# Softmax weights in a PSUM bank of their own, and GpSimd subtractions beside the products with v

## The chip, the cores and the metric

The kernel runs on one core of a Trainium2 chip. A core has a matrix engine (TensorE, PE in the profile), a vector engine (VectorE, DVE), an activation engine (ScalarE, ACT), a general engine (GpSimd, POOL) and a queue that issues transfers (SyncE, SP). TensorE writes its sums into PSUM, eight banks of 128 partitions with 512 fp32 values each; everything else works on SBUF, and transfers (DMA) go between SBUF and the chip's memory. The metric is the time of one execution on the device in microseconds (us), the median over several runs.

## The reference

The input x is 2048 x 640. Two branches are computed from it and mixed by a gate per row: attention with a short dilated window, and a dense layer, Mish and a second dense layer.

```python
def _A_ref(x, wqkv, wo):              # H = 32 heads of Dh = 20, W, dil = 8, 2
    qkv = (x @ wqkv).reshape(B, S, 3, H, Dh) ...
    idx = pos[:, None] - (arange(W) * dil)[None, :]      # 8 earlier rows, every second one
    logits = einsum("bhsd,bhswd->bhsw", q, k[idx]) * Dh ** -0.5   # -1e9 where idx < 0
    attn = softmax(logits, axis=-1)
    o = einsum("bhsw,bhswd->bhsd", attn, v[idx])
    return o.reshape(B, S, D) @ wo
def _B_ref(x, w1, b1, w2):            # F = 1728
    h = x @ w1 + b1
    return (h * tanh(softplus(h))) @ w2
g = sigmoid((x * gate_w).sum(-1))
return g * _A_ref(...) + (1 - g) * _B_ref(...)
```

## The kernel before, in words

**Precision.** Each fp32 matrix operand is split into a high and a low part, both in the format that TensorE takes at full speed: ScalarE copies it (the high part, line 345), and VectorE or GpSimd subtracts that from the original (the low part, line 348, function `split`). A tile "pair" holds both. One product is then three matmuls (`mm3`, lines 394 to 396): high by high, high by low, low by high. Some splits are made without a subtraction on an engine: ScalarE writes the negated copy and a transfer adds the source to it in flight (`split_added`, issued by GpSimd, line 357). Other additions in flight are issued by GpSimd too: those of the activations (`plus`, line 657) and of the results (`adding`, line 1066).

**Stages.** `qkv` forms q, k and v with x as the stationary operand, for 8 units u = 0..7: 4 groups of 8 heads (hq) times two halves of the rows (P). `mlp1` forms the first dense layer, and Mish is taken on ScalarE (line 669). In both, one PSUM bank takes 15 matmuls, and ScalarE drains it. `mlp2` is the second dense layer, in seven products named a, b, c, e, g, d, f that each run over seven blocks kc; a product keeps its accumulations in banks named p0, p1, q, u0, u1, w0, w1, r, v0, v1, for two halves P. `wo_first` and `wo_second` multiply the attention's result by wo, the first for row blocks tb 0 and 1, the second for tb 2 and 3. In `wo_second` five output blocks dc of tb 2 and the first three of tb 3 are begun with the operands kc 0 to 2, which are there early (`EARLY = 3`), then those of tb 2 are finished with kc 3 and 4, then the other two of tb 3 are begun, and then tb 3 is finished. `finish` adds a bank to the gated result of the other branch on VectorE (line 1282) and stores it.

**Attention** runs on VectorE beside the matmuls, function `attention`. Per unit there are two halves of four slots, and in each half: q by k for two slots at a time (line 451), the sum over a head's 20 elements (line 454, the kind "qk sum"), the maximum, the subtraction and the exponential on ScalarE, a copy of the weights into `pw` on ScalarE (`copied`, line 474), their sum, its reciprocal and the gate, and the scaling of `pw` by them (function `shares`, line 482). Then `outputs` multiplies v by the weights for two slots at a time (line 488, 2560 elements per partition, the weights repeated over a head's 20 elements), and three additions (lines 493, 494, 496) sum over the window. `out` transposes four slots (line 407) and stores them, for `wo_first` and `wo_second` to load.

**The order of the work** is worked out before the program is emitted, by a list planner (class `Plan`). Every piece of work is a task with an engine, an assumed duration, a rank and the tasks it waits for; the planner plays the engines forward and emits each task when it starts one. For each engine it takes the lowest rank among the ready tasks whose buffers are free; TensorE's tasks all have rank 0 and so go in the order written, past those that are not ready or have no free bank. Buffers come from rings, banks among them (`"bank": 8`). Attention has ranks from 2 - 0.6 on and comes behind the splits (`SOON` = 0, `NEXT` = 1).

Tasks of the engine "ANY" (most splits, and the sums of weight blocks of `sums_of`, lines 751 and 764) may go to VectorE or GpSimd. While attention is under way, VectorE takes one only when it is due: its matmul less than `NEAR` = 8000 ns off in TensorE's order, or, for tasks without one, after a wait (`PATIENCE`). GpSimd takes one only if it would end, by the planner's times, at most 150 ns after a "quiet" time, which is set when VectorE starts an instruction of the kind "qk sum". Whatever GpSimd starts in a quiet time, additions in flight included, is given a wait on the VectorE instruction ahead of the quiet one (`gate`, set through `follow`). The lines in `Plan.run`:

```python
fit = [t for t in fit if now + t.ns[0] <= quiet + 150 or t.rank <= -0.5]
...
if e == "POOL" and on and quiet > now and gate and ins:
    self.follow(ins, gate)
if e == "DVE":
    ...
    if t.kind == "qk sum":
        quiet, gate = now + t.ns, last
```

Of the kernel before, what the change touches and what calls it, by code (L numbers as in the profile page):

```python
# [8 lines left out]
F32 = mybir.dt.float32  # L9
F32R = mybir.dt.float32r  # L10
AF = mybir.ActivationFunctionType
OP = mybir.AluOpType
AX = mybir.AxisListType
PSUM = bass.MemoryType.PSUM
DRAM = bass.MemoryType.DRAM

S, D, H, DH, W, F = 2048, 640, 32, 20, 8, 1728
KC = D // 128
NQ, HQ = 4, 8
# [7 lines left out]
BIG = 1e9  # L27
WARM, WARM_TAIL = 6, 4
WA = 256

# [27 lines left out]
class Plan:  # L60


    NEAR, PATIENCE = 8000, 2000

    LAG = {"PE": 220, "ACT": 220, "DVE": 200, "POOL": 150, "SP": 3000}
    FAR, ROOM = 25000, 5000
# [29 lines left out]
    def run(self):  # L96
# [5 lines left out]
        quiet, gate, last, shared, begun = 0.0, None, None, [], False  # L102
# [33 lines left out]
        while left:  # L136
            again = not events or events[0][0] > now
            while again:
                again = False
                for e in self.LAG:  # L140
                    if busy[e]:
                        continue
                    fit = [t for t in ready[e] if fits(t)]
                    on = begun and loud
                    if e == "POOL":
                        fit += [t for t in shared if fits(t)]
                        if on:
                            fit = [t for t in fit if now + t.ns[0] <= quiet + 150 or t.rank <= -0.5]
                    elif e == "DVE":
                        fit += [t for t in shared if fits(t) and (not on or due(t))]  # L150
                    if not fit:
                        continue
                    t = min(fit, key=lambda t: t.key)
                    if t.both:
                        shared.remove(t)
                        t.eng = e
                    else:
                        ready[e].remove(t)
                    if type(t.ns) is tuple:
                        t.ns = t.ns[e == "DVE"]  # L160
                    for b in t.take:
                        b.ring.free -= 1
                        b.ring.at += 1
                        b.t = b.make()
                    t.start = now
                    ins = t.fn(e) if t.both else t.fn()
# [3 lines that stand above are left out]
                        if t.kind:  # L170
                            begun = True
                            loud -= 1
                        if t.kind == "qk sum":
                            quiet, gate = now + t.ns, last
                        last = ins or last
                    if e == "PE":
                        begun_pe = max(begun_pe, t.pos)
                    busy[e] = again = True
                    end = over = now + t.ns * self.CARE.get(e, 1.0)
                    heapq.heappush(events, (over, n, "idle", e))  # L180
                    if t.land:
                        wire = max(wire, end) + t.land
                        end = wire + (0 if e == "SP" else self.ADDING)
                    heapq.heappush(events, (end + self.LAG[e], n + 1, "done", t))
                    if e != "SP":
                        heapq.heappush(events, (over, n + 2, "own", t))
                    n += 3
            if not events:
                stuck = [(t.eng, t.rank, t.waits, getattr(t.fn, "__qualname__", "")) for e in ready for t in ready[e]]
                raise RuntimeError(f"nothing can go on at {now}, {left} left: {stuck[:20]}")  # L190
            now, _, what, x = heapq.heappop(events)
            if what == "idle":
                busy[x] = False
                continue
            if what == "ready":
                (shared if x.both else ready[x.eng]).append(x)
                continue
            if what == "done":
                left -= 1
                x.at = now  # L200
                for b in x.hold:
                    b.left -= 1
                    if not b.left:
                        b.ring.free += 1
                        if b.gone:
                            b.gone()
            for t in x.then:

                if (t.eng == x.eng and x.eng != "SP") != (what == "own"):
                    continue  # L210
                t.waits -= 1
                if not t.waits:
                    t.why, t.rdy = x, now
                    late = self.ROOM if x.eng == "SP" and t.eng == "ACT" and first[t] - begun_pe > self.FAR else 0
                    heapq.heappush(events, (now + max(t.late, late), n, "ready", t))
                    n += 1
# [4 lines left out]
def kernel(ctx: ExitStack, tc: tile.TileContext, x, wq, wo, w1, b1, w2, xt, gw, out):  # L221
    nc = tc.nc
    scale = DH ** -0.5
    V, G, A = nc.vector, nc.gpsimd, nc.scalar

    keep = ctx.enter_context(tc.tile_pool(name="keep", bufs=1))
    dram = ctx.enter_context(tc.tile_pool(name="dram", bufs=1, space=DRAM))
    psum = ctx.enter_context(tc.tile_pool(name="psum", bufs=8, space=PSUM))
    top = ctx.enter_context(tc.tile_pool(name="top", bufs=1, side="right"))
    pe = ctx.enter_context(tc.tile_pool(name="pe", bufs=1, side="right"))  # L230
    at = ctx.enter_context(tc.tile_pool(name="at", bufs=1))
# [1 line left out]
    NPAIR, NW, NRAW, NH = 21, 3, 7, 4  # L233
    def follow(ins, gate):
        tc.add_manual_dep(ins.ins, gate.ins.name,
                          mybir.DependencyInfo(mybir.DependencyClass.Sync, mybir.DependencyReason.DATA), reason="beside")

    plan = Plan({"bank": 8, "pair": NPAIR, "w": NW, "raw": NRAW, "raw1": 1, "hb": NH,
                 "ot": 1, "b": 11}, follow)

    def ps_buf():
# [75 lines left out]
    lg_w = lg.rearrange("p s h w -> p s w h")  # L317
    pw = at.tile([128, 8, W, HQ], F32, name="pw")
    pw_h = pw.rearrange("p s w h -> p s h w")
    pr = at.tile([128, 2, W, QF], F32, name="pr")  # L320
    mx = at.tile([128, 8, HQ], F32, name="mx")
    sm = at.tile([128, 8, HQ], F32, name="sm")
# [108 lines left out]
    def attention(u, P, hq, ready, gates):  # L431
# [44 lines left out]
        def shares(a, rank, e, copied):  # L476
            h = slice(a, a + 4)
            step = chain(rank)
            t = step("DVE", 415, lambda: V.tensor_reduce(sm[:, h], lg[:, h], op=OP.add, axis=AX.X), [e])
            step("DVE", 390, lambda: V.reciprocal(sm[:, h], sm[:, h]))  # L480
            step("DVE", 230, lambda: V.tensor_tensor(sm[:, h], sm[:, h], gate[:, P, h, None].to_broadcast([128, 4, HQ]), op=OP.mult), gates)
            return t, step("DVE", 430, lambda: V.tensor_tensor(pw[:, h], pw[:, h], sm[:, h, None, :].to_broadcast([128, 4, W, HQ]), op=OP.mult), [copied])

        def outputs(s0, rank, after):
            def mul():
                vw = window(kv, s0, 1)
                vw = bass.AP(tensor=vw.tensor, offset=vw.offset, ap=[list(d) for d in vw.ap[:3]] + [[DH, HQ], [1, DH]])
                V.tensor_tensor(pr.rearrange("p s w (h d) -> p s w h d", d=DH), vw,  # L488
                                pw[:, s0:s0 + 2, :, :, None].to_broadcast([128, 2, W, HQ, DH]), op=OP.mult)

            step = chain(rank)
            step("DVE", 2850, mul, after, kind="pv")
            step("DVE", 1495, lambda: V.tensor_tensor(pr[:, :, 0:4], pr[:, :, 0:4], pr[:, :, 4:8], op=OP.add), kind="pv")  # L493
            step("DVE", 855, lambda: V.tensor_tensor(pr[:, :, 0:2], pr[:, :, 0:2], pr[:, :, 2:4], op=OP.add), kind="pv")

            return step("DVE", 525, lambda: V.tensor_tensor(q[:, s0:s0 + 2], pr[:, :, 0], pr[:, :, 1], op=OP.add), kind="pv")
# [16 lines left out]
        for i, a in enumerate((4, 0)):  # L513
            h = 2 * u + i
# [3 lines left out]
            e, copied = softmax(a, LATER - 0.6, [bounded(a, a + 4, [t1, t2])], used)  # L518
            summed, w = shares(a, turn_of(h, 1), e, copied)
# [39 lines left out]
    def qkv(u, P, hq):  # L559
# [4 lines left out]
        if u == 0:  # L564
            last = warmed
            for kc in range(2):
                (xh, xl), (wh, wl) = X[0, kc].ready, WQ[0, kc].ready
                for a, b, w in ((0, 0, [xh, wh]), (0, 1, [wl]), (1, 0, [xl])):
                    slots = range(4)
                    if (kc, a, b) == (0, 0, 0):  # L570

                        for c0, c1, wc in ((0, WA, WQ[0, 0].first), (WA, n, wh)):
                            last = pe_add(2 * mm_ns(n // 2), lambda c0=c0, c1=c1: nc.tensor.matmul(
# [738 lines left out]
    def first_in():  # L1312
# [5 lines left out]
        WQ[0, 0] = wp  # L1318
        cols = ((0, WA), (WA, NCOL))
        d = [dma(lambda c0=c0, c1=c1: wr.t[:, c0:c1], lambda c0=c0, c1=c1: wq[0, 0][:, c0:c1], rank=-1.5, take=[wr] if not c0 else (),  # L1320
                 hold=[wr], size=(c1 - c0) * 512) for c0, c1 in cols]
        hi = [add("ACT", act_ns(WA), lambda: A.activation(wp.t[:, 0, :WA], wr.t[:, :WA], AF.Copy), d[:1], rank=SOON, take=[wp], hold=[wr]),
              add("DVE", 250, lambda: V.tensor_copy(wp.t[:, 0, WA:NCOL], wr.t[:, WA:NCOL]), d[1:], rank=-1.1, hold=[wr, wp])]
# [129 lines left out]
```

## Time and profile before

| what | us |
|---|---|
| median of 3 runs | 631.64 (631.42 to 632.35) |
| span of the profiled execution | 630.2 |
| TensorE busy | 625.6 (99%) |
| VectorE busy | 581.0 (92%) |
| ScalarE busy | 333.5 (53%) |
| GpSimd busy | 143.4 (23%) |

The profiled execution's own time is its span, 630.2 us from the first to the last instruction; the run's time has a little around that, and the median of the runs is 631.64 us. In the rows that follow, a group of instructions is named by its line, its engine, its operation and the tiles it writes and reads (out<-in), with count, busy time in us and the mean of one in ns; what stands after the second bar is the engine's idle time just before them. A row of waits names who waited for whom, the time in total, how often, and the longest. A row of the timeline begins with start and duration in us.

### The profile page before, as it was taken

How to read it: one execution, taken by the hardware profiler on the slowest of the kernel's cores; microseconds unless marked ns; L12 is line 12 of the kernel's file. 1: busy time of each engine (PE TensorE's matmuls, PEld its weight loads, DVE VectorE, ACT ScalarE, POOL GpSimd, SP SyncE). 2: the span in 40 equal slices, each digit the busy share in tenths (PEclk: the TensorE clock that was granted, in tenths of full speed). 3: DMA queues.
4: the chain of work that ended last, by engine and by line, in shares of the span. 5: the costliest groups of instructions: out<-in, count | busy, mean ns of one | idle time of the engine just before them, and what ended most of it. 6: DMA issues, size and time to landing. Idle time of an engine off the chain costs nothing.

```text
span 630.2 us, 8823 instructions
## 1 busy us (share of the span) xinstructions
PE 625.6 (99%) x2794; PEld 521.9 (83%) x2794; DVE 581.0 (92%) x610; ACT 333.5 (53%) x705; POOL 143.4 (23%) x154
## 2 busy tenths in 40 slices
PE   9999999999999999999999999999999999999997
PEld 6888888888888888888888888888888888888886
DVE  7699989999999998998999899999999989999934
ACT  6665764454536645353652626683765536666300
POOL 1321242232312332331333341211201010002320
PEclk9999999999999999999999999999999999999999
DMA  9999998999977998895898798899989867799985
GB/s 321 344 338 225 180 271 210 317 256 274 269 206 175 322 313 195 209 271 112 186 324 185 150 290 196 216 322 287 298 275 287 231 222 252 231 340 322 253 236 189
DMA packets 105694, 159.12 MB, mean 253 GB/s; under 512 B 13728, under 2 KB 52768, under 8 KB 105360
## 3 DMA queue, kind: packets, MB, share of 16 engines
q1 hardware_dynamic: 89648, 131.74, 64.1%
q0 software_dynamic: 15712, 26.56, 27.3%
q8 instruction: 22, 0.36, 0.2%
q10 hardware_dynamic: 288, 0.26, 0.1%
q14 instruction: 24, 0.20, 0.1%
HBM read 95.27 MB, written 67.51 MB: 258 GB/s over the span
## 4 chain that ended last, share of the span: by engine, by line
PE 98%; DMA 1%; ACT 0%; SPq 0%; DVE 0%; issue 0%
PE bank L395 32%; PE bank L394 32%; PE bank L396 32%; DMA hb<-in_x 1%; PE bank L400 1%; PE bank L401 1%; PE bank L546 0%; SPq L362 0%; ACT kvq L345 0%; ACT pair L345 0%; DVE kvq L1282 0%
## 5 line engine op out<-in xcount | busy, mean ns | idle before, releaser
L395 PE MATMUL bank<-pair 128*128 128x512 f32 (+1 forms) x500 | 193.1, 386 | 0.0
L394 PE MATMUL bank<-pair 128*128 128x512 f32 (+1 forms) x500 | 193.1, 386 | 0.0
L396 PE MATMUL bank<-pair 128*128 128x512 f32 (+1 forms) x500 | 193.1, 386 | 0.0
L396 PEld LDWEIGHTS bank<-pair 128*128 128x128 f32 x500 | 93.9, 188 | 18.1
L394 PEld LDWEIGHTS bank<-pair 128*128 128x128 f32 x500 | 93.9, 188 | 18.1
L395 PEld LDWEIGHTS bank<-pair 128*128 128x128 f32 x500 | 93.9, 188 | 17.9
L488 DVE TENSOR_TENSOR pr<-kvq,pw 128x2560 f32<-128x2560 f32 x32 | 91.7, 2865 | 1.0
L451 DVE TENSOR_TENSOR pr<-kvq 128x2560 f32<-128x2560 f32 x32 | 91.0, 2843 | 0.9
L454 DVE TENSOR_REDUCE lg<-pr 128x128 f32<-128x2560 f32 x32 | 90.2, 2819 | 0.7
L345 ACT ACTIVATE pair<-raw 128x512 fp32r<-128x512 f32 (+3 forms) x120 | 70.5, 611 | 33.4 <-DMA raw<-o 18.1
L552 ACT ACTIVATE kvq<-bank 128x320 f32<-128x320 f32 x64 | 28.0, 438 | 82.9 <-PE bank L396 82.4
L394 PE MATMUL bank<-pair,w 128*128 128x512 f32 x182 | 70.8, 389 | 0.0
L395 PE MATMUL bank<-pair,w 128*128 128x512 f32 x182 | 70.8, 389 | 0.0
L396 PE MATMUL bank<-pair,w 128*128 128x512 f32 x182 | 70.8, 389 | 0.0
L348 DVE TENSOR_TENSOR pair<-raw,pair 128x512 fp32r<-128x512 f32 (+2 forms) x103 | 67.1, 678 | 2.7 <-ACT pair L345 2.6
L669 ACT ACTIVATE hb<-bank,bias 128x512 f32<-128x512 f32 x52 | 35.6, 688 | 59.2 <-PE bank L396 55.7
L395 PE MATMUL bank<-pair,kvq 128*128 128x496 f32 (+2 forms) x149 | 56.4, 378 | 0.0
L394 PE MATMUL bank<-pair,kvq 128*128 128x496 f32 (+2 forms) x149 | 56.4, 378 | 0.0
L396 PE MATMUL bank<-pair,kvq 128*128 128x496 f32 (+2 forms) x149 | 56.4, 378 | 0.0
L345 ACT ACTIVATE pair<-hb 128x512 fp32r<-128x512 f32 (+3 forms) x62 | 37.9, 611 | 23.8 <-DMA hb<-actt 12.3
L657 POOL DMA_DIRECT2D actt<-actt x28 | 26.7, 965 | 95.7 <-DMA actt<-actt 53.5
L493 DVE TENSOR_TENSOR pr<-pr 128x1280 f32<-128x1280 f32 x32 | 47.5, 1486 | 0.3
(130 smaller groups left out, 896.8 us busy)
## 6 DMA issues: line engine op xcount, KB each, us to landing
actt<-hb SPq DMA_DIRECT2D x52, 256.0 KB, 6.3
act<-hb SPq DMA_DIRECT2D x38, 256.0 KB, 6.1
raw<-actt SPq DMA_DIRECT2D x35, 256.0 KB, 4.1
raw<-act SPq DMA_DIRECT2D x30, 256.0 KB, 4.9
actt<-hb POOLq DMA_DIRECT2D x26, 256.0 KB, 6.8
actt<-actt POOLq DMA_DIRECT2D x24, 256.0 KB, 6.0
kvq<-in_xt SPq DMA_DIRECT2D x16, 320.0 KB, 7.0
o<-ot SPq DMA_DIRECT2D x64, 80.0 KB, 4.3
```

What stands on the lines that cost most here:

```text
L345: a = add("ACT", act_ns(n), lambda: A.activation(hi(), raw(), AF.Copy), after, rank=rank, take=take, hold=hold)
L348: return (V if e == "DVE" else G).tensor_tensor(lo(), raw(), hi().bitcast(F32), op=OP.subtract)
L394: nc.tensor.matmul(ps, ah, bh, start=first, stop=False, skip_group_check=more)
L395: nc.tensor.matmul(ps, ah, bl, start=False, stop=False, skip_group_check=more)
L396: nc.tensor.matmul(ps, al, bh, start=False, stop=last, skip_group_check=more)
L451: return V.tensor_tensor(pr, window(kv, s0, 0), q[:, s0:s0 + 2, None, :].to_broadcast([128, 2, W, QF]), op=OP.mult)
L454: V.tensor_reduce(lg_w[:, s0:s0 + 2], pr.rearrange("p s w (h d) -> p s w h d", d=DH), op=OP.add, axis=AX.X)
L488: V.tensor_tensor(pr.rearrange("p s w (h d) -> p s w h d", d=DH), vw, pw[:, s0:s0 + 2, :, :, None].to_broadcast([128, 2, W, HQ, DH]), op=O ...
L493: step("DVE", 1495, lambda: V.tensor_tensor(pr[:, :, 0:4], pr[:, :, 0:4], pr[:, :, 4:8], op=OP.add), kind="pv")
L552: a = add("ACT", 330, lambda: A.activation(kv[:, 7 + s], ps.t[:, QF:3 * QF].rearrange("p (a b) -> p a b", a=2), AF.Copy), [done] + before, ...
L657: return add("POOL", 1200, lambda: G.dma_start(out=blk[key][:rows], in_=src(), accum_op=OP.add, max_dma_last_dim=2048), after, rank=-0.5, ...
L669: a = add("ACT", 595, lambda: A.activation(to(it()), src(), AF.Mish, bias=bias[:n, fc:fc + 1]), after + [bias_in], rank=NEXT, take=[] if h ...
```

## The change

Three things are changed together. One PSUM bank is taken out of the ring of the matmuls, which keeps seven, and becomes a tile `pg` in a pool of its own. The scaling of the weights on VectorE (`shares`) writes `pg` in place of `pw`, and the product with v (`outputs`) reads `pg`, so that one of its two operands lies in PSUM. And the product gets a kind of its own, "pv mul", that opens a quiet time in the planner as "qk sum" does, so that GpSimd may start shared work beside it.

```diff
+NBANK = 7
...
+    QUIET = ("qk sum", "pv mul")
...
-                        if t.kind == "qk sum":
+                        if t.kind in self.QUIET:
                             quiet, gate = now + t.ns, last
...
-    psum = ctx.enter_context(tc.tile_pool(name="psum", bufs=8, space=PSUM))
+    psum = ctx.enter_context(tc.tile_pool(name="psum", bufs=NBANK, space=PSUM))
+    shared = ctx.enter_context(tc.tile_pool(name="shared", bufs=1, space=PSUM))
...
-    plan = Plan({"bank": 8, "pair": NPAIR, "w": NW, "raw": NRAW, "raw1": 1, "hb": NH,
+    plan = Plan({"bank": NBANK, "pair": NPAIR, "w": NW, "raw": NRAW, "raw1": 1, "hb": NH,
                  "ot": 1, "b": 11}, follow)
...
     pw = at.tile([128, 8, W, HQ], F32, name="pw")
     pw_h = pw.rearrange("p s w h -> p s h w")
+    pg = shared.tile([128, 8, W, HQ], F32, name="pg")
...
-            return t, step("DVE", 430, lambda: V.tensor_tensor(pw[:, h], pw[:, h], sm[:, h, None, :].to_broadcast([128, 4, W, HQ]), op=OP.mult), [copied])
+            return t, step("DVE", 430, lambda: V.tensor_tensor(pg[:, h], pw[:, h], sm[:, h, None, :].to_broadcast([128, 4, W, HQ]), op=OP.mult), [copied])
...
                 V.tensor_tensor(pr.rearrange("p s w (h d) -> p s w h d", d=DH), vw,
-                                pw[:, s0:s0 + 2, :, :, None].to_broadcast([128, 2, W, HQ, DH]), op=OP.mult)
+                                pg[:, s0:s0 + 2, :, :, None].to_broadcast([128, 2, W, HQ, DH]), op=OP.mult)
...
-            step("DVE", 2850, mul, after, kind="pv")
+            step("DVE", 2850, mul, after, kind="pv mul")
```

## The prediction, made before the change was run

> **What bounds the kernel now.** I read the page's busy shares and its chain first, then the busy time of the engines by stretches, then the groups by form, and last the timeline of the end. The page:
>
> ```profile
> span 630.2 us, 8823 instructions
> PE 625.6 (99%) x2794; PEld 521.9 (83%) x2794; DVE 581.0 (92%) x610; ACT 333.5 (53%) x705; POOL 143.4 (23%) x154
> PE 98%; DMA 1%; ACT 0%; SPq 0%; DVE 0%; issue 0%
> ```
>
> TensorE (PE) is busy in 625.6 of 630.2 us, and the chain that ended last runs through it for 98%. A busy PE need not be a PE at its peak, since the records of neighbouring matmuls overlap; so the next rows give busy time with the number of instructions in brackets. The first three are of PE alone; the other three hold PE, PEld, DVE, ACT, POOL in this order.
>
> ```profile
> 450.00:500.00 50.00, 50.00 (x222) 1.00 0.91 281
> 500.00:600.00 100.00, 100.00 (x442) 1.00 0.88 264
> 8.00:626.00 618.00, 618.00 (x2765) 1.00 0.92 253
> ...
> 30.00:600.00 570.00, 570.00 (x2541) 476.74 (x2540) 549.00 (x568) 311.70 (x656) 132.31 (x143) 1.00 0.93 250
> 400.00:600.00 200.00, 200.00 (x884) 165.65 (x883) 192.46 (x264) 116.32 (x215) 27.69 (x31) 1.00 0.90 274
> ```
>
> From 8 to 626 us there is no idle time of PE at all, at a granted clock of 1.00. In 450 to 500 a matmul goes off every 50/222 = 0.225 us, in 500 to 600 every 0.226, in 400 to 600 every 200/884 = 0.226: one pace, so no stall hides under the overlap of the records. PE sets the end, and what it does is fixed: 2794 matmuls, before and after. All that a change of the other engines can win lies at the two ends:
>
> ```profile
> 0.79 3.12 PE L330 MATMUL bank<-const-bfloat16-1.0 128*128 128x512 bf16 x10 [0.79 <-PEq L1441]
> 4.41 0.38 PE L573 MATMUL bank<-pair,kvq 128*128 128x240 f32 x1 [0.33 <-DVE pair L1323]
> 7.66 1.60 PE L546 MATMUL bank<-pair,kvq 128*128 128x496 f32 x6 [0.22 <-ACT pair L345]
> ...
> 626.94 0.42 DVE L1282 TENSOR_TENSOR kvq<-bank,kvq 128x256 f32<-128x256 f32 x1 [0.29 <-PE bank L396]
> ```
>
> In front stand 0.79 us before the warm-up, 0.33 and 0.22 us; behind stand 630.2 - 627.4 = 2.8 us, in which the last block is stored. The change touches none of these.
>
> **The change part by part.** The costs come from these groups (count, then busy us and mean ns) and the summary of line L488; the windows below them are L488's alone (busy DVE, count).
>
> ```profile
> L488 DVE TENSOR_TENSOR pr<-kvq,pw 128x2560 f32<-128x2560 f32 x32 | 91.7, 2865 | 1.0
> L348 DVE TENSOR_TENSOR pair<-raw,pair 128x512 fp32r<-128x512 f32 x88 | 59.4, 697 | 2.7 <-ACT pair L345 2.6
> L482 DVE TENSOR_TENSOR pw<-pw,sm 128x256 f32<-128x256 f32 x16 | 7.3, 457 | 1.3
> L927 DVE TENSOR_TENSOR kvq<-kvq,bank 128x512 f32<-128x512 f32 x8 | 5.5, 683 | 1.5 <-PE bank L401 0.8 <-PE bank L396 0.7
> L1282 DVE TENSOR_TENSOR raw<-bank,raw 128x512 f32<-128x512 f32 x5 | 3.5, 692 | 13.5 <-PE bank L396 13.5
> L943 DVE TENSOR_TENSOR raw<-raw,w 128x512 f32<-128x512 f32 x5 | 3.3, 678 | 0.0
> L751 DVE TENSOR_TENSOR raw<-raw 128x256 f32<-128x256 f32 x8 | 3.3, 413 | 1.2 <-DMA raw<-in_w 1.2
> L764 DVE TENSOR_TENSOR raw<-raw 128x512 f32<-128x512 f32 x3 | 2.1, 684 | 0.0
> L751 DVE TENSOR_TENSOR raw<-raw 128x128 f32<-128x128 f32 x3 | 0.9, 284 | 0.0
> L927 DVE TENSOR_TENSOR kvq<-kvq,raw 128x512 f32<-128x512 f32 x2 | 1.4, 684 | 0.0
> ...
> L488 DVE TENSOR_TENSOR pr<-kvq,pw x32: 2817/2825/3986, 69.1 to 583.7; 128x2560 f32<-128x2560 f32 x32
> ...
> 60.00:400.00 340.00, 71.93 (x25) 1.00 0.93 234
> 400.00:600.00 200.00, 19.75 (x7) 1.00 0.90 274
> ```
>
> *1. The products with v read their weights from PSUM (32 instructions, L488).* A vector instruction with one operand in a bank takes 683 ns against 684 with both in SBUF (L927), and 692 against 678 in another pair of lines (L1282, L943). So the difference is -1 to +14 ns an instruction: -0.03 to +0.45 us over 32 if it is fixed, and five times that, -0.2 to +2.2 us, if it grows with 2560 elements against 512. I take 0, since the first pair differs in the bank alone. [...]
>
> *2. The scaling of the weights writes to PSUM (16 instructions, L482).* No row shows DVE writing a bank. The nearest are the reads above: 14 ns up or down, 0.2 us over 16; doubled durations would be 16 x 457 ns = 7.3 us, the upper end. I take 0. What waits for it is the product on the same engine, and PE waits for neither.
>
> *3. GpSimd may start beside the products.* Two operands in SBUF collide with GpSimd; one in a bank does not:
>
> ```profile
> 358.81 2.56 POOL L348 TENSOR_TENSOR pair<-raw,pair 128x512 fp32r<-128x512 f32 x2
> 360.07 3.99 DVE L488 TENSOR_TENSOR pr<-kvq,pw 128x2560 f32<-128x2560 f32 x1
> ...
> 610.41 0.69 DVE L1282 TENSOR_TENSOR raw<-bank,raw 128x512 f32<-128x512 f32 x1 [8.47 <-PE bank L396]
> 610.62 1.30 POOL L943 TENSOR_TENSOR raw<-raw,w 128x512 f32<-128x512 f32 x1
> ```
>
> The product at 360.07 took 3.99 us instead of the median 2.825, behind a GpSimd subtraction. At 610.6 a GpSimd product ran in 1.30 us beside a DVE addition with a bank operand, which kept its 0.69. So what the planner moves beside a product costs DVE nothing. What can move: up to 400 us only the 8 + 3 sums of L751 and 3 of L764 that DVE does now, 3.3 + 0.9 + 2.1 = 6.3 us; from 400 us on 7 products, at two 1.3 us subtractions under each 2.8 us, 14 splits of L348 at 697 ns, 9.8 us. With 91.7 - 32 x 2.825 = 1.3 us of collisions gone, DVE loses up to 17.4 us of its 581.0, and I expect half to all of it (572 to 564). GpSimd gains 14 x 1.3 = 18 us and the sums, some 30 us on 143.4.
>
> What that is worth: DVE stands idle 570 - 549.0 = 21 us in 30 to 600 already and holds up no matmul. Its relief lies wholly under PE: 0 us. Attention may end some us earlier, and nothing waits for that either.
>
> *4. Waits added.* Whatever GpSimd starts in a product's window, additions by DMA too, now waits for the DVE instruction ahead of the product; the rest of GpSimd's queue stands behind it. Those additions feed the sums of products (actt) and the results (r). At these two places GpSimd waits now already, and PE doesn't notice:
>
> ```profile
> POOL actt L657 <- ACT w L669: 13.4, 1, 13.4
> POOL actt L657 <- DMA actt<-w: 11.0, 2, 7.3
> ...
> L348 POOL TENSOR_TENSOR pair<-raw,pair x17: 1007/1294/2374, 26.4 to 609.4; 128x512 fp32r<-128x512 f32 x10, 128x384 fp32r<-128x384 f32 x7
> L348 POOL TENSOR_TENSOR pair<-hb,pair x4: 1282/1296/1418, 25.0 to 450.2; 128x512 fp32r<-128x512 f32 x4
> ...
> ACT kvq L552 <- PE bank L396: 82.4, 41, 2.7
> ```
>
> (The last three rows are for this and the next parts: 17 + 4 splits are on GpSimd already, and 41 times ACT sat idle until PE had filled a bank of q, k and v.) The added waits are taken at 0, because the planner starts a shared subtraction at the latest when its matmul is 8 us off (NEAR) and DVE runs in the planner's order. If that cover is gone: the rival below.
>
> *5. Seven banks in place of eight.* Up to `mlp2` a bank is filled by 15 matmuls, 3.4 us, so with seven ACT has 6 x 3.4 = 20 us to drain one, and by the 41 waits above it mostly stands ready. In `mlp2` at most six accumulations are open (p0, p1, q for two halves), or four and four that drain while the next start. The place with eight is `wo_second`: five blocks of dc for tb 2 and three for tb 3, nine matmuls each, opened one behind the other.
>
> ```profile
> 595.20 0.69 DVE L348 TENSOR_TENSOR pair<-raw,pair 128x512 fp32r<-128x512 f32 x1
> 595.80 0.69 DVE L348 TENSOR_TENSOR pair<-hb,pair 128x512 fp32r<-128x512 f32 x1
> ...
> 615.10 0.68 DVE L348 TENSOR_TENSOR pair<-hb,pair 128x512 fp32r<-128x512 f32 x1
> ```
>
> The first bank is read at 610.41 (above), 8.47 us after DVE went idle, when block (2, 0) had its last six matmuls. So (2, 0) went on at 610.4 - 6 x 0.226 - 0.2 = 608.85, and 72 matmuls before it give 592.6 for the first and 606.8 for the eighth block. With seven banks that eighth block must wait until (2, 0) is drained. The planner then takes the next product that can run: (2, 0) with its late operands, whose splits ended at 595.80 + 0.69 = 596.5, 10.3 us ahead. Six matmuls later (1.36 us) and a 0.69 us addition after that its bank is free. PE only changes the order: 0 us. Upper end: without those operands PE would stand from 606.8 to 611.1, 4.3 us.
>
> **Sum.** 630.2 us of the profiled execution + 0 (PE's work) + 0 (ends) + 0 to 1 us of small stalls in a new order: 630.2 to 631. The runs' median, 631.64, lies 1.4 us over the span, so I forecast 631.8. 0.2% of it, 1.26 us, is about what a measurement of this kernel can tell from no change.
>
> **The rivals.**
> *Slower: a split on GpSimd comes late.* A subtraction that the planner now gives to GpSimd may stand behind an addition that waits. With the waits above it would start 7.3 or 13.4 us late and take 1.3 us; with 8 us in hand PE then stops for 0.6 or 6.7 us, and one such place at the middle gives 3.7, so 635.3 us. It decides from 9.3 us of lateness. For it: the last split of the kernel (615.10) is there only 4.3 us before the end products, which are 30 matmuls' worth (6.8 us) back from 626.9, at 620.1; and every order of work from 69 us on changes. Against it: GpSimd is busy 23%, and 21 splits sit in the same queue now without a stop. The dearer value would need the longest wait and the least margin together.
> *Slower: the eighth bank is missed.* 4.3 us as worked out, 636.1, if the late operands of tb 2 come over 10.3 us later; against it, DVE is relieved and reaches them sooner.
> *The change doesn't do what it says:* PSUM weights leave the port as it is. Then each of 28 moved operations costs the product 3.99 - 2.825 = 1.16 us, 32 us on DVE against 16 saved; the 16 more fit in its 21 idle us, so still about 632. The row at 610.41 speaks against it. [...]
> *Faster.* Earlier attention could only win where PE is idle, and the gaps of the start are 1.3 us together, before any attention: at best 630.3, if all went.
>
> **Chances.** Forecast 0.76; late split 0.14; eighth bank 0.04; port as it is 0.03; faster 0.03. The first and the fourth come out the same: 0.79 within 0.2%, 0.03 faster, 0.18 slower. The likeliest case's own range is 630.9 to 632.9. For 8 in 10 the range reaches past it to the cheaper late splits: 2.2 us over the forecast, halfway between the cheapest (0.6) and the middle one (3.7), is 634.0. Left out are the dearer half of the late splits, the bank's case and a gain.
>
> **What would show it.** PE: 10.00 us busy in each 10 us up to 620 and 0.226 us a matmul; one stretch with fewer matmuls refutes the sum, and what its PE waits for (a pair written by POOL, or a bank read by DVE) tells the rivals apart. L488: mean near 2825 and no 3986. POOL: subtractions beside L488, L751 gone from DVE, L348 on POOL from 21 to 30 or more. DVE: 564 to 572 us. End: block (3, 2) begins after (2, 0). The prediction is wrong if the new order leaves PE without an operand for over 1.3 us.

## The result and the profile after

The changed kernel takes 639.14 us (median of 4 runs, 636.44 to 640.45) against 631.99 us before: ratio 1.011, 95% interval 1.0091 to 1.0129. It is slower by 1.1%, and lies outside the predicted range. The profiled execution is the run of 639.04 us; its page:

```profile
span 637.3 us, 8841 instructions
PE 629.2 (99%) x2794; PEld 523.1 (82%) x2794; DVE 577.9 (91%) x570; ACT 330.2 (52%) x705; POOL 195.2 (31%) x194
PE 73%; DVE 11%; DMA 10%; issue 3%; ACT 1%; SPq 1%; POOL 1%; DVEq 0%; ACTq 0%; POOLq 0%
```

GpSimd took 40 pieces of work from VectorE (570 instructions against 610) and is busy 52 us longer; VectorE is relieved of only 3 us. The chain that ended last, 98% PE before, is now 73% PE, and the rest of it runs mostly through VectorE (11%) and transfers (10%). The span is 7.1 us longer. Where the time is lost is seen in the busy times of PE, PEld, DVE, ACT and POOL by stretches of 10 us, here of the changed kernel:

```profile
540.00:550.00 10.00, 10.00 (x46) 8.26 (x45) 10.00 (x13) 7.91 (x15) 4.81 (x3) 1.00 0.54 165
550.00:560.00 10.00, 6.81 (x27) 4.85 (x26) 10.00 (x9) 3.25 (x6) 9.39 (x6) 0.95 0.68 208
560.00:570.00 10.00, 10.00 (x41) 8.10 (x40) 9.94 (x16) 5.18 (x9) 4.82 (x4) 0.88 0.86 254
```

and of the kernel before:

```profile
540.00:550.00 10.00, 10.00 (x46) 8.29 (x45) 9.81 (x17) 7.39 (x13) 0.00 (x0) 1.00 0.89 277
550.00:560.00 10.00, 10.00 (x46) 8.29 (x45) 8.88 (x17) 6.92 (x13) 0.00 (x0) 1.00 1.03 351
560.00:570.00 10.00, 10.00 (x46) 8.29 (x45) 10.00 (x18) 7.26 (x14) 0.90 (x1) 1.00 1.00 333
```

Between 550 and 560 us TensorE issues 27 matmuls in place of 46, VectorE gets 9 instructions done in place of 17 while busy all the time, and GpSimd, idle there before, works 9.39 us. The next rows show what TensorE waited for behind its start, in the whole execution, and then its matmuls around the two longest stops (start, duration, and in brackets the idle time before and what ended it):

```profile
PE bank L400 <- DVE pair L353: 2.3, 1, 2.3
PE bank L400 <- POOL pair L353: 1.6, 2, 0.9
```

```profile
552.71 0.39 PE L399 MATMUL bank<-pair 128*128 128x512 f32 x1
554.01 0.50 PE L400 MATMUL bank<-pair 128*128 128x512 f32 x1 [0.92 <-POOL pair L353]
...
555.28 0.39 PE L399 MATMUL bank<-pair 128*128 128x512 f32 x1
557.94 0.50 PE L400 MATMUL bank<-pair 128*128 128x512 f32 x1 [2.27 <-DVE pair L353]
```

The second matmul of a product, high by low, waits for the low part: once from GpSimd, once from VectorE. Without a stop a matmul follows the one before after 0.23 us (0.226 in 400 to 600 us of the kernel before, at a granted clock of 1.00; no run has the operands in another format, so "full speed", as said of the format, means this pace here), so from start to start the two cost 1.30 - 0.23 = 1.1 us and 2.66 - 0.23 = 2.4 us. There is a further cost behind them. The stretches of PE alone around 559 us (busy, count, granted clock):

```profile
553.00:559.00 6.00, 2.81 (x12) 1.00 0.62 210
559.00:562.40 3.40, 3.40 (x10) 0.50 0.85 256
562.40:566.00 3.60, 3.60 (x17) 1.00 0.86 223
```

For 3.4 us the clock is granted at half, which costs 1.7 us. With a third stop at 488 us (0.9 us from start to start, shown further down), 0.25 us at 585 and a start that was 0.4 us later, this is 6.7 of the 7.1 us.

Why both engines are slow there is seen in the timeline; first the changed kernel, VectorE and then GpSimd:

```profile
551.06 1.77 DVE L948 TENSOR_TENSOR kvq<-kvq,w 128x512 f32<-128x512 f32 x1
552.76 1.75 DVE L948 TENSOR_TENSOR w<-w 128x512 f32<-128x512 f32 x1
554.43 1.78 DVE L948 TENSOR_TENSOR kvq<-kvq,w 128x512 f32<-128x512 f32 x1
556.14 1.75 DVE L353 TENSOR_TENSOR pair<-hb,pair 128x512 fp32r<-128x512 f32 x1
...
552.24 3.42 POOL L353 TENSOR_TENSOR pair<-raw,pair 128x512 fp32r<-128x512 f32 x2
555.62 3.42 POOL L353 TENSOR_TENSOR pair<-hb,pair 128x512 fp32r<-128x512 f32 x2
```

and VectorE in the kernel before at the same place:

```profile
553.00 0.69 DVE L348 TENSOR_TENSOR pair<-hb,pair 128x512 fp32r<-128x512 f32 x1
...
555.48 0.69 DVE L943 TENSOR_TENSOR kvq<-kvq,w 128x512 f32<-128x512 f32 x1
```

Instructions of the same kind, with two operands in SBUF each, take 1.75 us where they took 0.69, and GpSimd's take 1.71 where 1.29 is usual: the engines hold each other up here. The planner was meant to keep GpSimd away from such work. Its bar (`on = begun and loud`) holds while steps of attention are left, and those end much earlier now. The last addition over the window, before (L496) and after (L501; lines are 5 further down in the changed kernel):

```profile
L496 DVE TENSOR_TENSOR kvq<-pr x32: 484/492/495, 74.5 to 594.8; 128x320 f32<-128x320 f32 x32
```

```profile
L501 DVE TENSOR_TENSOR kvq<-pr x32: 482/492/496, 78.6 to 544.8; 128x320 f32<-128x320 f32 x32
```

Before, attention ended at 595 us, when almost all splits were done. After, it ends at 545, and from then on the planner gives GpSimd any shared work at any time, counted at its undisturbed duration, in a stage that has VectorE full and its splits just ahead of the matmuls.

### The profile page after: what moved, and what is told of

Read it like the earlier page. It is cut to its first block, busy times and chain, and to the rows that moved or that the text cites. A ratio compares the mean times of both kernels' runs of the same rounds, so it can differ in the third digit from the quotient of the medians.

```text
span 637.3 us, 8841 instructions
## 1 busy us (share of the span) xinstructions
PE 629.2 (99%) x2794; PEld 523.1 (82%) x2794; DVE 577.9 (91%) x570; ACT 330.2 (52%) x705; POOL 195.2 (31%) x194
## 4 chain that ended last, share of the span: by engine, by line
PE 73%; DVE 11%; DMA 10%; issue 3%; ACT 1%; SPq 1%; POOL 1%; DVEq 0%; ACTq 0%; POOLq 0%
PE bank L400 24%; PE bank L401 24%; PE bank L399 24%; DVE pair L353 6%; DMA hb<-actt 3%; DMA raw<-s 2%; DMA raw<-actt 1%; DMA raw<-act 1%; DMA hb<-s 1%; DMA hb<-in_x 1%; DMA r<-hb 1%; DVE lg L459 1%; DVE pr L498 1%; SPq L367 1%; DMA r<-kvq 1%
## 5 line engine op out<-in xcount | busy, mean ns | idle before, releaser
L493 DVE TENSOR_TENSOR pr<-kvq,pg 128x2560 f32<-128x2560 f32 x32 | 90.2, 2819 | 1.0
L353 DVE TENSOR_TENSOR pair<-raw,pair 128x512 fp32r<-128x512 f32 (+2 forms) x85 | 64.3, 775 | 5.2 <-ACT pair L350 5.1
L353 POOL TENSOR_TENSOR pair<-raw,pair 128x512 fp32r<-128x512 f32 (+1 forms) x35 | 49.7, 1445 | 59.7 <-DMA r<-hb 20.0
L557 ACT ACTIVATE kvq<-bank 128x320 f32<-128x320 f32 x64 | 28.1, 438 | 71.5 <-PE bank L401 71.3
```

The lines of the kernel that those rows point to most:

```text
L353: return (V if e == "DVE" else G).tensor_tensor(lo(), raw(), hi().bitcast(F32), op=OP.subtract)
L557: a = add("ACT", 330, lambda: A.activation(kv[:, 7 + s], ps.t[:, QF:3 * QF].rearrange("p (a b) -> p a b", a=2), AF.Copy), [done] + before, ...
```

## The experiments

The theory after the comparison is **G** (the guard, that is, the bar on GpSimd): VectorE's relief ends attention 50 us earlier, and with it the bar that keeps GpSimd away from VectorE's two-operand work. The rivals: **B**, the bank (seven for matmuls, or VectorE's access to the eighth) costs the time; **W**, the splits under the products with v come late in GpSimd's queue.

**The bank without the quiet times.**

```diff
-    QUIET = ("qk sum", "pv mul")
+    QUIET = ("qk sum",)
```

> Weights in PSUM and seven banks as in the changed kernel, but only the sums (qk sum) open a quiet time. Theory G (the loss comes from GpSimd's subtractions: relieved attention ends some 50 us earlier, and from then on the planner lets GpSimd subtract beside VectorE's two-operand work): little is moved, attention ends at about 595 us as before, 631.5 to 633 us. Rival B (seven banks, or reading and writing the bank on VectorE, cost the time): 636 to 640 us.

Measured: 631.77 us against 631.87, ratio 1.0001 (0.9992 to 1.0011). Its page and its group of the product:

```profile
span 630.0 us, 8821 instructions
...
L493 DVE TENSOR_TENSOR pr<-kvq,pg 128x2560 f32<-128x2560 f32 x32 | 90.2, 2820 | 1.0
```

The product with its weights in the bank takes 2820 ns, as the undisturbed one of before (2825). Seven banks and VectorE's work on the eighth cost nothing here; B falls. (So in this run VectorE works on a bank: it reads it in 2820 ns a product and writes it in 437 ns a scaling. ScalarE works on banks too, as it drains them: 436 ns for 128x320 at L557.)

**The bar kept to the end.** GpSimd may take shared work outside quiet times no more, even when attention has ended.

```diff
                     if e == "POOL":
                         fit += [t for t in shared if fits(t)]
-                        if on:
+                        if begun:
                             fit = [t for t in fit if now + t.ns[0] <= quiet + 150 or t.rank <= -0.5]
```

> The changed kernel, but GpSimd stays barred from shared work outside quiet times after attention has ended too; VectorE takes it at once there. Theory G: no subtraction on GpSimd after the last product with v, TensorE's stop at 552 to 562 us and the half clock behind it go, 632 to 634 us, with the stop of 1 us at 488 us perhaps left. Rival W (the splits under the products come late because they stand in GpSimd's queue): still 636 to 640 us. Rival B: still 636 to 640 us.

Measured: 634.08 us against 631.87 (10 runs, 632.03 to 637.42), ratio 1.0041 (1.0024 to 1.0058). Some 5 of the 7 us are back although attention ends at 543 us, as early as without this edit, so G holds for them and W falls for them. About 2.2 us are left, with a wide spread, at the upper edge of what was expected. The profiled execution is the longest of the ten; its last addition of attention and its stops:

```profile
L501 DVE TENSOR_TENSOR kvq<-pr x32: 481/492/493, 74.0 to 543.2; 128x320 f32<-128x320 f32 x32
...
PE bank L399 <- ACT w L1168: 2.5, 1, 2.5
PE bank L400 <- POOL pair L353: 1.1, 1, 1.1
```

The second, at 488 us, is one of the changed kernel's too; from start to start it costs 1.2 us here. The first, at 584 us, hangs on a transfer of weights that landed late: ScalarE waited 3.9 us for it. In the changed kernel ScalarE waited 0.3 us for a load of the same weights, at 585 us. How often such a load is late enough to stop TensorE is not known, since the other nine runs have no trace; so about 1 of the 2.2 us of the median is not located.

**The bar lifted early in the kernel before.** Eight banks, weights in SBUF, the old quiet times; only `on`, and the bar with it, ends when seven steps of the products with v are left.

```diff
-                    on = begun and loud
+                    on = begun and loud > 7
```

> The kernel before (eight banks, weights in SBUF, no new quiet times), but GpSimd's bar ends when seven steps of the products with v are still to come, which is some 50 us before the end of attention. Theory G: subtractions of 0.69 us on VectorE grow to 1.75 us beside GpSimd's, TensorE stops in 545 to 600 us, 634 to 640 us. Rivals W and B: nothing they name is in it, 631.5 to 632.5 us.

Measured: 647.46 us against 631.87, ratio 1.0256 (1.0239 to 1.0273). TensorE's waits:

```profile
PE bank L395 <- DVE pair L348: 9.6, 4, 5.0
PE bank L401 <- DVE pair L348: 0.6, 1, 0.6
PE bank L395 <- POOL pair L348: 0.6, 1, 0.6
```

Nothing of the change is in this kernel, and the early end of `on` alone slows it, by more than expected (15.6 us against 2 to 8). The longest stop is 5.0 us, and the mean granted clock is 0.992, which is 0.008 of 645.7 us, 5.2 us. Steps of attention lie among the collisions here, until 582 us, and some are slowed too; that this is why it costs more is argued, not shown. Two things end with `on` in this edit, as they do in the changed kernel: the bar on GpSimd, and the rule that VectorE takes shared work only when it is due. The run before, which put back the bar alone, tells them apart. The end of `on` is enough by itself to stop TensorE.

**The quiet times without the bank.**

```diff
-                        if t.kind == "qk sum":
+                        if t.kind in ("qk sum", "pv mul"):
...
-            step("DVE", 2850, mul, after, kind="pv")
+            step("DVE", 2850, mul, after, kind="pv mul")
```

> The kernel before (eight banks, weights in SBUF) with the products with v as quiet times. The port theory: both operands in SBUF, so each subtraction beside a product costs it up to 1.16 us, L488's mean goes from 2.87 to 3.3 us or more and VectorE loses what it is relieved of; attention ends later than in the changed kernel, 632 to 637 us. If PSUM doesn't matter to the port: L488 stays at 2.87 us and the time is that of the changed kernel, 637 to 640 us.

Measured: 650.46 us against 631.87, ratio 1.0298 (1.0273 to 1.0323). The product, GpSimd's splits, and TensorE's main waits:

```profile
L488 DVE TENSOR_TENSOR pr<-kvq,pw 128x2560 f32<-128x2560 f32 x32 | 98.6, 3083 | 1.0
L348 POOL TENSOR_TENSOR pair<-raw,pair 128x512 fp32r<-128x512 f32 x27 | 51.8, 1924 | 55.4 <-DMA r<-hb 18.6 <-ACT pair L345 11.1 <-DVE pair L348 9.8
...
PE bank L395 <- POOL pair L348: 4.9, 4, 2.8
PE bank L395 <- DVE pair L348: 3.4, 4, 2.1
```

The product rises to 3083 ns, less than the 3300 expected; GpSimd waits too, with 1924 ns a split against 1514 in the changed kernel. Both numbers fall by the bank, so it does what the change says. The time was set too low: neither theory had 650, since I priced VectorE's loss and not the stops that late low parts of either engine make. Most of the loss comes ahead of the end of attention, which is at 554 us here: TensorE's 2401st matmul starts at 552.7 us, against 540.6 in the kernel before, so 12 of the 16.4 us are lost by then. The end of the bar has the smaller share.

**What is left, first try: additions in flight planned later.** In the changed kernel the stop at 488 us looks like this (GpSimd, VectorE, TensorE):

```profile
485.70 0.82 POOL L1071 DMA_DIRECT2D ot<-ot  x1 [6.42 <-DMA ot<-ot]
486.24 1.32 POOL L353 TENSOR_TENSOR pair<-raw,pair 128x384 fp32r<-128x384 f32 x1
487.24 1.55 POOL L353 TENSOR_TENSOR pair<-hb,pair 128x512 fp32r<-128x512 f32 x1
...
482.51 2.82 DVE L493 TENSOR_TENSOR pr<-kvq,pg 128x2560 f32<-128x2560 f32 x1
486.32 3.03 DVE L353 TENSOR_TENSOR pair<-hb,pair 128x512 fp32r<-128x512 f32 x1
...
487.75 0.39 PE L399 MATMUL bank<-pair 128*128 128x512 f32 x1
488.85 0.50 PE L400 MATMUL bank<-pair 128*128 128x512 f32 x1 [0.70 <-POOL pair L353]
```

The two subtractions of GpSimd were meant for the product at 482.51 to 485.33. They stood behind an addition in flight that waited until 485.70 for the one before it to land, and so they left the quiet time. The second came late for TensorE (488.85 - 487.75 - 0.23 = 0.9 us), and both together held up a subtraction of VectorE for 3.03 - 0.68 = 2.35 us. Theory **Q** (the queue): such places are the rest. The planner took 6 us for an addition to land; this run, with the bar kept, takes 9.

```diff
-    ADDING = 6000
+    ADDING = 9000
```

> The kernel with the bar kept (e2), and the planner now takes 9 us instead of 6 for an addition in flight to land, so that what depends on one is planned later. Theory Q (what is left of the loss, 634.1 against 631.9 us, comes from subtractions that stand in GpSimd's queue behind an addition that waits, leave their quiet time and stop a subtraction of VectorE for 2 to 4 us): the two long subtractions on VectorE at 443 and 486 us go, and the time is 631.5 to 633 us. Rival D (attention's early end shifts transfers, and late loads stop TensorE): the stops stay, 633 to 636 us.

Measured: 632.06 us against 632.00, ratio 1.0003 (0.9994 to 1.0012). The same place, then VectorE's splits as a group and the last addition of attention:

```profile
477.29 0.82 POOL L1071 DMA_DIRECT2D ot<-ot  x1 [5.76 <-DMA ot<-ot]
479.47 1.03 POOL L353 TENSOR_TENSOR pair<-raw,pair 128x384 fp32r<-128x384 f32 x1 [1.35 <-DVE pg L487]
480.45 1.30 POOL L353 TENSOR_TENSOR pair<-hb,pair 128x512 fp32r<-128x512 f32 x1
...
479.27 2.82 DVE L493 TENSOR_TENSOR pr<-kvq,pg 128x2560 f32<-128x2560 f32 x1
483.08 0.69 DVE L353 TENSOR_TENSOR pair<-hb,pair 128x512 fp32r<-128x512 f32 x1
...
L353 DVE TENSOR_TENSOR pair<-raw,pair 128x512 fp32r<-128x512 f32 x81 | 54.5, 697 | 4.2 <-ACT pair L350 4.1
...
L501 DVE TENSOR_TENSOR kvq<-pr x32: 480/492/494, 76.8 to 536.9; 128x320 f32<-128x320 f32 x32
```

Now the addition is off before the product begins, both subtractions lie under it and end by 481.75, and VectorE's subtraction takes 0.69 us. The other long one, 4.25 us at 444 us in the changed kernel, is gone too. The splits' mean is 697 ns as before the change, at 81 instead of 88. Q holds: with the additions planned later the loss is gone. D, late loads because attention ends early, falls as far as the early end alone is meant: attention ends at 537 us here, and no load stops TensorE. The edit moves everything that depends on an addition, though, so it is not shown that the late load at 584 us of the run before came from the queue.

**What is left, second try: no splits under the products.** With the bar kept and 6 us for additions.

```diff
...
+                    if e == "POOL" and soft and quiet > now:
+                        fit = [t for t in fit if not t.both or t.need is None]
...
-                            quiet, gate = now + t.ns, last
+                            quiet, gate, soft = now + t.ns, last, t.kind == "pv mul"
```

> The kernel with the bar kept (e2), but beside the products with v GpSimd may take only shared work that no matmul waits for soon (the sums of weight blocks); splits go there only beside the sums of qk, as in the kernel before. Theory Q: no splits beyond those of the kernel before, no long subtraction on VectorE in 400 to 545 us, 631.5 to 633 us. Rival D: VectorE is relieved of the sums alone, about 5 us, attention ends at 585 to 595 us and nothing shifts, 631.5 to 633 us as well; so this run tells whether the splits under the products are needed for what is left, the one before tells which way they act.

Measured: 632.12 us against 632.00, ratio 1.0001 (0.999 to 1.0012). One subtraction of VectorE still takes 1.42 us, at 447 us, where no long one was expected, and attention ends at 587 us. So the splits under the products are needed for what was left; the run before has them, and shows no harm from them where they don't slip.

**The fourth corner: additions later, bar ending with attention.**

```diff
-    ADDING = 6000
+    ADDING = 9000
```

> The changed kernel with 9 us for the landing of additions, and with the bar on GpSimd ending with attention as in the changed kernel; the fourth corner beside the changed kernel (both causes), the bar kept (queue alone) and both mended. Two separate causes: the stops at about 488 us are gone, VectorE's subtractions of 1.75 us after attention's end are there, 635 to 638 us. If the end of the bar only hurts a VectorE that the queue has made late already: 632 to 633 us.

Measured: 634.76 us against 632.03 (7 runs, 632.73 to 635.82), ratio 1.0039 (1.0024 to 1.0055), just under the 635 to 638 expected of two separate causes. Two of VectorE's rows behind attention's end (538 us):

```profile
544.97 1.78 DVE L932 TENSOR_TENSOR kvq<-kvq,raw 128x512 f32<-128x512 f32 x1
546.67 1.78 DVE L948 TENSOR_TENSOR w<-w 128x512 f32<-128x512 f32 x1
```

The collisions are there as in the changed kernel, and the loss is 2.7 us instead of 7. So the queue alone costs 2.2 us and the end of the bar alone 2.7 us. With both mended nothing is lost, and both together cost 7.15 us: 2.2 us more than the sum, with an uncertainty of about 1.9 us by the intervals of the three measurements. A part of that is the clock. Its mean granted value is 0.997 in all four runs of the changed kernel, which is 0.003 of 637 us, 1.9 us; it is below 0.999 in none of these seven runs and in one of the ten with the bar kept. That the rest is the margin that the queue takes from the splits before the collisions begin is argued, not shown.

No version beats the kernel before, and none could by this road while the matmuls are the floor: the best leave TensorE as gapless as it was.

## Why the prediction was wrong

*What bounds the kernel* was right: the matmuls are the floor, nothing was won, and the three variants whose traces show no such stop (the bank without the quiet times, the bar kept with additions later, and no splits under the products) lie at 631.8 to 632.1 us.

*Parts 1 and 2* were right: a product takes 2819 ns (median before 2825), and a scaling that writes the bank 433 ns. The mean before, 457 ns, held one of 933; the median before was 426, so writing the bank costs 7 ns, 0.1 us over 16.

*Part 3* is the step that failed, at its last sentence: "Attention may end some us earlier, and nothing waits for that either." It ended 50 us earlier, and the planner's bar on GpSimd hung on it: `on` falls with the last step of attention, as the code told. What was put at 0 cost some 5 of the 7 us (the run with the bar kept), 2.7 us by itself. I priced the collision (1.16 us, with rows for it) only beside the products with v, and took the relieved VectorE as one whose matmuls are safer, where the relief itself opened the stage to the same collision. The sentence "what the planner moves beside a product costs DVE nothing" held for what stayed beside a product. VectorE's busy time came to 577.9 us where 564 to 572 was expected, and to 573.1 with the bar kept.

*Part 4* failed as well: the wait was named and the sum took 0, where the runs show 2.2 us when it acts alone. The cover of 8 us that the 0 rested on was not there. GpSimd's late subtraction was meant to end with its product, by about 485.5 us, and its matmul could have started at 487.75 + 0.23 = 488.0, so the cover was some 2.5 us, an estimate from these rows; a wait of 6.42 us, shorter than the 7.3 of the rival, was enough. The rival itself, a split behind an addition that waits, was right as a mechanism. What it left out is a second price: the slipped subtraction not only comes late itself (0.9 us, within 0.6 to 6.7), it stands in VectorE's way as well, for 2.35 us here. Its chance was 0.14, and it was one of two causes; its middle value of 635.3 us is near what the queue alone gives (634.1), but the 639.1 us came from both.

*Part 5* was right: the run of the bank without the quiet times has seven banks, and in its trace TensorE waits for no bank and no operand. In the changed kernel the first bank of the last stage is drained at 615.5, and PE does not stop there.

*The range* held the forecast and one cheap stop; it had no term for two causes at once, nor for the clock.

## What to carry to other kernels

In a kernel whose bottleneck never idles, freeing another engine can win nothing; ask what the freed engine's earlier end switches: a guard, a phase, a condition in a scheduler. When work is moved into a window on a queue that is worked in order (as GpSimd's two subtractions here stood behind an addition until 485.70 us), ask what stands ahead of it there, and what it collides with if it leaves the window. A planner's durations hold only for the overlap they were measured in (0.69 us was 1.75 here).

## What the runs showed of the hardware that was not expected

**The clock.** TensorE's granted clock fell to half for 3.4 us after a stop of 2.27 us (with one of 0.92 us 3 us ahead of it), and after one of 2.49 us in the run with the bar kept:

```profile
585.40:588.80 3.40, 3.40 (x10) 0.51 1.05 406
```

In these two the low stretch began 1.0 and 1.4 us after the matmuls had resumed. In the run of the quiet times without the bank, with longest stops of 2.8 and 2.1 us, the mean granted clock is 0.994, and in the run with the bar lifted early, with a longest stop of 5.0 us, it is 0.992, against 0.999 to 1.000 in the runs of the kernel before. Single stops of up to 1.1 us had no such stretch behind them: after the one of 0.70 us at 488 us the changed kernel has 1.00 from 489 to 500 us; with the bar kept, the mean of 0.997 is 1.9 us lost in 635.6, of which the stretch above is 1.7, so that another behind the stop of 1.1 us has no room; and with additions later and the bar ending with attention, the longest stop is 0.8 us and the mean 1.000. From what length of a stop on the clock falls, and what sets the 3.4 us, no run shows.

**VectorE beside GpSimd** (the prediction and the expectations call it the port; the runs show the times, not what lies behind them). Two operands in SBUF on VectorE beside a GpSimd subtraction: 0.69 us becomes 1.75, and GpSimd's 1.29 becomes 1.71, VectorE's starts lying 1.67 to 1.71 us apart (551.06, 552.76, 554.43, 556.14). With two GpSimd subtractions one behind the other (486.24 to 488.79), one VectorE subtraction that began at 486.32 took 3.03 us. With one operand in a bank, neither was slowed in the run with additions planned later: 2.82 us for the product and 1.30 us for the subtraction under it.
